# Accumulating scatters of a top-2 mixture of experts, placed one at a time; another form for the last expert

## The chip, the core and the metric

One NeuronCore of a Trainium2 chip runs the whole program. The metric is the device time of one execution in microseconds, the median of several runs. TensorE (PE) multiplies matrices, VectorE (DVE) and ScalarE (ACT) work elementwise, GpSimd (POOL) computes elementwise as well and issues the DMAs whose rows are chosen by an index (gathers and scatters), and SyncE (SP) issues the other DMAs. Each engine takes its own instructions strictly in order.

## The reference, cut to what matters

Attention and a gated feed-forward layer give 2304 tokens of 512 numbers. A mixture of eight experts follows; every token goes to two of them, and the result of a token is the weighted sum of the two:

```python
top2 = np.argpartition(-noisy_logits, 2, axis=1)[:, :2]
...
out = np.zeros((N, D), dtype=np.float32)
for e in range(E):
    for k in range(2):
        mask = top2[:, k] == e
        ...
        h = np.maximum(x[mask] @ w1[e], 0.0)
        out[mask] += top2_w[mask, k, None] * (h @ w2[e])
```

Here E is 8, x[mask] has 512 columns, w1[e] is 512 x 1024 and w2[e] is 1024 x 512.

## The kernel before, in words

The gate scatters each token's row, its weights and its number into `xs`, a region in device memory for each expert (`g_scatter`, L620, plain scatters of 96 rows). An expert then has up to 640 of its rows in five tiles of 128 (the fifth has 104 for experts 2 to 7).

Experts 0 and 1 are done in 32 units (`units`, L1151): 16 slices of 128 hidden columns in two parts of the tokens, "a" with three tiles and "b" with two. Units 0 to 7 are expert 0's part a, 8 to 15 expert 1's a, 16 to 23 expert 1's b, 24 to 31 expert 0's b. A unit makes the up products of its slice (`up2`), the down products of the unit before (`down2`), and splits the weights of the unit two ahead into a high and a low half (`prep2`, ACT then DVE).

Experts 2 to 7 are done in 24 pairs of slices (`pair`, L1068), four to an expert. A pair multiplies two slices at once in a Strassen-like scheme of seven products (`product`, L1048), which needs sums and differences of weight blocks (`sums_ws`, on POOL, L1010 to L1013) and of the turned rows (`sums_xs`, on POOL), split into halves by ACT (`high_ws`, L1028) and DVE (`low_ws`, L1032). Among the products stand the down products of the pair before (`down_s`, L1062). The sums for pair p + 1 are issued at the start of pair p.

An expert's five tiles sum in five banks of PSUM. `finish` (L920) multiplies a tile by the tokens' weights into a buffer `pv`, and `add` (L931) issues a scatter on POOL that adds the 128 rows into `out` in device memory. Every scatter into `out` waits until the one before has landed, since the rows of two may be the same. For experts 2 to 6 `finish` runs in the first pair of the next expert, and issues its scatters at once: three, then two.

Side work has its place by hand: `put(("u", n), h, fn, ...)` or `then` places a call in unit n at step h, `at(p, h, fn, ...)` in pair p, and `run` issues what is due, in the order of h.

Of the kernel before, what the change touches and what calls it, by code (L numbers as in the profile page):

```python
# [14 lines left out]
AF = mybir.ActivationFunctionType  # L15
OP = mybir.AluOpType
# [8 lines left out]
E = 8  # L25
# [31 lines left out]
NC = CAP // 128  # L57
# [10 lines left out]
def moe_program(ctx, tc, phi, kv, q, wa, wgn, nz, wb, out):  # L68
# [10 lines left out]
    V, A, P, G, Q = nc.vector, nc.scalar, nc.tensor, nc.gpsimd, nc.sync  # L79
# [560 lines left out]
    def put(i, n, fn, *a):  # L640
        fill.setdefault((i, n), []).append((fn, a))
# [38 lines left out]
    for b in range(1, B):  # L680
        i = 2 * b - 2
        n = AT["s1"][min(b, 2)]
# [187 lines left out]
    def rows(e, part):  # L870
        if "all" not in PV:
            PV["all"] = wpool.tile([128, 8, DM], F32, tag="X0", name="pv", bufs=1)
            PV["next"], PV["ring"] = 0, 3
        for t in TILES[part]:
            PV[e, t] = PV["all"][:, PV["next"], :]
            PV["next"] = (PV["next"] + 1) % PV["ring"]
# [40 lines left out]
    def height(e, t):  # L917
        return CAPS - 128 * t if e > 1 and t == NC - 1 else 128

    def finish(e, tiles, late=False, engines="AV"):  # L920
        ml = ML[e]
        for t in tiles:
            pv, h = PV[e, t], height(e, t)
            if engines[t % len(engines)] == "V":
                V.tensor_scalar(pv[:h], AC2[e, t][:h], ml[:h, t, e:e + 1], None, op0=OP.mult)
            else:
                A.activation(pv[:h], AC2[e, t][:h], AF.Copy, scale=ml[:h, t, e:e + 1])  # L927
            if not late:
                add(e, t)

    def add(e, t):  # L931

        h = height(e, t)
        G.indirect_dma_start(out=out, out_offset=bass.IndirectOffsetOnAxis(ap=IX[e][:h, t:t + 1], axis=0),  # L934
                             in_=PV[e, t][:h], in_offset=None, compute_op=OP.add)


    A11, A12, A22, S1, S2, S3, S4 = range(7)
# [113 lines left out]
    def down_s(p, n, tiles):  # L1052
        e, f = 2 + p // 4, 2 * (p % 4) + n
        hh, hl = HS[p, n]
        w = W2[24 + 2 * p + n]
        for t in tiles:
            h = height(e, t)
            if f == 0:
                AC2[e, t] = bank((0, 1, 4, 2, 3)[t], [128, DM], "acc")
            o = slice(128 * t, 128 * t + h)  # L1060
            for m, (a, b) in enumerate(((hh, 0), (hh, 1), (hl, 0))):
                P.matmul(AC2[e, t][:h], r(a[:, o]), r(w[:, b]), start=(f == 0 and m == 0),  # L1062
                         stop=(f == NF2 - 1 and m == 2))
# [95 lines left out]
    def then(s, f, part, half, fn, *a):  # L1159
        put(("u", pos[s, f, part]), half, fn, *a)  # L1160

    def then_x(s, f, part, e, k, a):
        then(s, f, part, 1, trans_x, e, k, a)
        then(s, f, part, 2.1, split_x2, e, k, a)
# [9 lines left out]
        then(0, 6 + k // 2, "a", 1.5 * (k % 2), trans_x, 1, k, "a")  # L1174
        then(0, 6 + k // 2, "a", (1, 2.1)[k % 2], split_x2, 1, k, "a")
    then(1, 0, "a", 1, index, 1, "a")
    then(1, 0, "a", 1.5, finish, 0, TILES["a"], True)
    for t in TILES["a"]:
        then(1, (0, 1, 1)[t], "a", (1.6, 0.5, 1.5)[t], add, 0, t)
    then(1, 2, "a", 0.5, rows, 1, "a")  # L1180
    put(("u", 10), 0.3, swap)
    put(("u", 10), 0.3, load_x, 1, "b")
    then(1, 5, "a", 2.1, index, 1, "b")
    for k in range(4):
        then(1, 6 + k // 2, "a", (1, 2.1)[k % 2], trans_x, 1, k, "b")
        then(1, 6 + k // 2, "a", (1.5, 2.2)[k % 2], split_x2, 1, k, "b")
    put(("u", 16), 0, open_s1)
    then(1, 0, "b", 1, load_x, 0, "b")
    then(1, 0, "b", 1.5, finish, 1, TILES["a"])
# [6 lines left out]
    then(2, 2, "b", 1.5, rows, 0, "b")  # L1196
    then(1, 0, "b", 1, load_xs, 2)
    for k in range(2):
        for n, (f, fn, m) in enumerate(((20, trans_xs, 0), (20, trans_xs, 1), (21, sums_xs, 0), (21, None, 0),
                                        (22, None, 1), (22, None, 2), (22, sums_xs, 1), (23, None, 3))):  # L1200
            f += (0, 4 + (n > 3))[k]
            h = (1, 2.1, 0.1, 1, 1, 1.1, 2.3, 1)[n]
            if fn:
                put(("u", f), h, fn, 2, k, m)
            else:
                put(("u", f), h, high_xs, 2, k, m)
                put(("u", f), h + 1.1, low_xs, 2, k, m)
# [6 lines left out]
    def at(p, h, fn, *a):  # L1214
        put(("s", p), h, fn, *a)

    pairs = 4 * (E - 2)
# [49 lines left out]
    open_s2()  # L1267
    for p in range(pairs):
        e, q = 2 + p // 4, p % 4
        if p == 0:  # L1270
            def first(h):
                if h == 0:
                    down2(*units[-1])
                    finish(0, TILES["b"], engines="A")
                    rows(2, "ab")

            def second(h):
                pass
        else:
            ends = p % 4 == 0  # L1280

            def first(h):
                down_s(p - 1, 0, (range(3), range(3, NC))[h])

            def second(h):
                t = (range(3), range(3, NC))[h]
                down_s(p - 1, 1, t)
                if ends:
                    finish(e - 1, t, engines="A")
                    if h:  # L1290
                        rows(e, "ab")
        pair(p, first, second)
    for t in range(NC):
        for n in range(2):
            down_s(pairs - 1, n, (t,))
        finish(E - 1, (t,), engines="AV")
    assert not fill, fill
    right.close()
    left.close()
# [78 lines left out]
```

## Time and profile before

| what | value |
|---|---|
| median of 3 runs | 998.56 us (997.41 to 999.58) |
| the profiled execution, its own time | 997.44 us |
| its span, first to last instruction | 995.6 us |
| PE busy | 852.6 us (86%) |
| DVE busy | 626.4 us (63%) |
| ACT busy | 394.8 us (40%) |
| POOL busy | 322.0 us (32%) |
| mean granted clock of TensorE | 0.933 of full speed |

The busy times are shares of the whole span. The attention and the first layer take the first 420 us or so, the units of experts 0 and 1 run from there to about 554 us, and the pairs from 554 us to the end.

### The profile page before, as it was taken

The numbers are of one execution on the slowest core, as the hardware profiler recorded it, in microseconds if no ns is written. First come the engines' busy times: TensorE is split into PE (matmuls) and PEld (weight loads), VectorE is DVE, ScalarE is ACT, GpSimd is POOL, SyncE is SP. The second block draws the span as 40 slices with busy tenths as digits, with TensorE's granted clock in tenths as the row PEclk, the third lists the DMA queues.
The fourth block names the chain that finished last, engine by engine and source line by source line (L and its number), as shares of the span: only waits on it lengthen the run. The fifth ranks groups of instructions, "written<-read, shape, count | busy, mean of one in ns | idle before, by whom it ended". The sixth has DMA issues, their size and how long they took to land. (4 is left out here: it accounts for less than half of the span.)

```text
span 995.6 us, 16514 instructions
## 1 busy us (share of the span) xinstructions
PE 852.6 (86%) x6136; PEld 746.5 (75%) x6136; DVE 626.4 (63%) x1498; ACT 394.8 (40%) x845; POOL 322.0 (32%) x438
## 2 busy tenths in 40 slices
PE   5989999999999999999897799579499399399490
PEld 2768888998999889887787688468378288288380
DVE  4775686767767685866465688278187187285340
ACT  3754554334433433434353445145145145244220
POOL 2000114242424244223224254353453442542302
PEclk9999999999999999999989899879889699699695
DMA  9966378753445346656692526417427237224203
GB/s 335 400 250 178 104 241 292 247 142 96 138 138 147 85 138 189 184 157 208 173 234 43 127 76 140 91 44 153 79 70 159 46 95 150 30 86 107 29 12 43
DMA packets 85002, 140.76 MB, mean 141 GB/s; under 512 B 16352, under 2 KB 41152, under 8 KB 84912
## 3 DMA queue, kind: packets, MB, share of 16 engines
q1 hardware_dynamic: 65712, 100.66, 33.1%
q0 software_dynamic: 19200, 38.96, 17.8%
q8 instruction: 50, 0.82, 0.3%
q14 instruction: 40, 0.33, 0.1%
HBM read 102.81 MB, written 36.77 MB: 140 GB/s over the span
## 5 line engine op out<-in xcount | busy, mean ns | idle before, releaser
L1048 PE MATMUL ph<-xh,ws 128*128 128x308 f32 x1008 | 168.4, 312 | 85.4 <-ACT ws L1028 71.2
L1048 PEld LDWEIGHTS ph<-xh,ws 128*128 128x128 f32 x1008 | 155.6, 193 | 101.1 <-ACT ws L1028 72.5
L1062 PE MATMUL acc<-ws,hs 128*128 128x512 f32 (+1 forms) x720 | 191.3, 409 | 0.0
L1062 PEld LDWEIGHTS acc<-ws,hs 128*128 128x128 f32 (+1 forms) x720 | 135.4, 194 | 27.5
L934 POOL DMA_INDIRECT out<-pv,ix x40 | 64.3, 1608 | 217.1 <-DMA out<-pv,ix 96.5
L459 PE MATMUL acc<-a,ro 128*128 128x288 f32 x576 | 116.3, 294 | 0.0
L426 PE MATMUL pg<-x,pt 128*128 128x288 f32 x576 | 103.3, 314 | 6.4 <-ACT pt L394 4.4
L459 PE MATMUL acc<-a,os 128*128 128x288 f32 x432 | 105.8, 294 | 0.8 <-DVE os L408 0.8
L1066 DVE SCALAR_TENSOR_TENSOR hs<-y,hs 128x308 fp32r<-128x308 f32 x72 | 42.7, 598 | 93.0 <-ACT hs L1104 89.8
L426 PEld LDWEIGHTS pg<-x,pt 128*128 128x128 f32 x576 | 82.3, 191 | 25.0 <-issue 7.6
L426 PE MATMUL pv<-x,pt 128*128 128x288 f32 x576 | 93.3, 298 | 0.0
L459 PEld LDWEIGHTS acc<-a,ro 128*128 128x128 f32 x576 | 92.1, 188 | 0.0
L426 PEld LDWEIGHTS pv<-x,pt 128*128 128x128 f32 x576 | 83.0, 191 | 0.0
L439 DVE SCALAR_TENSOR_TENSOR ta<-ta,pg 128x288 f32<-128x288 f32 x84 | 37.9, 451 | 66.5 <-ACT ta L434 61.7
L622 POOL DMA_INDIRECT xs<-R,gidx x48 | 49.0, 1022 | 89.5 <-DMA xs<-R,gidx 84.6
L418 POOL DMA_DIRECT2D os<-osl x72 | 40.6, 564 | 106.2 <-PE acc L459 62.7
L459 PEld LDWEIGHTS acc<-a,os 128*128 128x128 f32 x432 | 74.1, 188 | 1.1 <-DVE os L408 1.1
L434 ACT ACTIVATE ta<-pg 128x288 f32<-128x288 f32 x84 | 34.4, 410 | 88.2 <-PE pg L426 86.2
L1028 ACT ACTIVATE ws<-ts 128x512 fp32r<-128x512 f32 x46 | 28.6, 622 | 102.5 <-POOL ts L1011 102.3
L445 ACT ACTIVATE a<-ta 128x288 fp32r<-128x288 f32 x84 | 37.4, 445 | 72.1 <-DVE ta L440 66.2
L896 PE MATMUL ph<-xt,wm 128*128 128x384 f32 (+1 forms) x256 | 60.5, 322 | 5.6 <-ACT xt L858 4.0
L896 PEld LDWEIGHTS ph<-xt,wm 128*128 128x128 f32 x256 | 45.9, 195 | 11.2 <-ACT xt L858 6.0
(212 smaller groups left out, 1512.0 us busy)
## 6 DMA issues: line engine op xcount, KB each, us to landing
wb<-wb SPq DMA_DIRECT2D x72, 512.0 KB
os<-osl POOLq DMA_DIRECT2D x72, 256.0 KB, 3.5
stg<-wa SPq DMA_DIRECT2D x19, 511.8 KB
kv<-kv SPq DMA_DIRECT2D x32, 256.0 KB
xl<-xs SPq DMA_DIRECT2D x40, 160.0 KB
out<-zt SPq DMA_DIRECT2D x1, 5888.0 KB
xd<-R SPq DMA_DIRECT2D x8, 603.0 KB
qt<-q SPq DMA_DIRECT2D x8, 576.0 KB
```

What stands on the lines that cost most here:

```text
L418: G.dma_start(r(lo), r(osl[f][:, :]))
L426: P.matmul(p, r(PT[f // 2, g][:, w, f % 2, 128 * a:128 * a + 128]), r(X[i][:, s, g, :]), start=(g == 0 and n == 0), stop=(g == 1 and n == 2))
L434: A.activation(ta, pg, AF.Tanh, scale=0.5)
L439: V.scalar_tensor_tensor(ta, ta, 1.0, pg, op0=OP.add, op1=OP.mult)
L445: A.activation(r(ah[:, 0, :]), ta, AF.Copy)
L459: P.matmul(ACC[i][c], r(OS[i, f][w][:, o]), r(ah[:, s, :]), start=(f == 0 and n == 0), stop=(f == NF1 - 1 and n == 2))
L622: G.indirect_dma_start(out=xs[:, :], out_offset=bass.IndirectOffsetOnAxis(ap=RT[i][:, t, n:n + 1], axis=0), in_=R[i][:, t, :], in_offset=None)
L896: P.matmul(p, r(w[:, c]), r(x[:, k, b, :]), start=(m == 0), stop=(m == 11))
L934: G.indirect_dma_start(out=out, out_offset=bass.IndirectOffsetOnAxis(ap=IX[e][:h, t:t + 1], axis=0), in_=PV[e, t][:h], in_offset=None, com ...
L1048: P.matmul(out, r(w[:, i, c + 128 * k:c + 128 * k + 128]), r(x[:, m, k, a]), start=(start and n == 0), stop=(n == 5), skip_group_check=not ...
L1062: P.matmul(AC2[e, t][:h], r(a[:, o]), r(w[:, b]), start=(f == 0 and m == 0), stop=(f == NF2 - 1 and m == 2))
L1066: V.scalar_tensor_tensor(r(hl), y, 0.0, hh, op0=OP.max, op1=OP.subtract)
```

## The change

`finish` no longer issues scatters. It puts the tile on a list `todo`, and `add()` without arguments takes the oldest from it and issues its scatter. Eight such calls stand in the units (8, twice in 9, then 17, 19, 21, 27, 29), and two in every pair, at steps 2.5 and 5.9. All tiles are now scaled by ACT, where some were scaled by DVE.

The last expert is treated otherwise. In pair 23 five gathers (`gather`) read from `out` the rows to which its five tiles belong. At the end `finish` multiplies a tile by the weights and adds the gathered rows in one DVE instruction, and a plain scatter (`OP.bypass`) writes the sum to `out`. The down products of pair 22 for tiles 3 and 4 are held back from pair 23 to the very end, after the down products of pair 23 for tiles 0 to 2.

Two placements of other work move as well. The turned rows of expert 1's part b (`trans_x`, `split_x2`) go from units 14 and 15, two in each, to units 12 to 15, one in each. Some transposes, sums and splits of expert 2's rows in units 20 to 29 move by up to one unit.

```diff
-    def finish(e, tiles, late=False, engines="AV"):
+    todo = []
+
+    def finish(e, tiles):
         ml = ML[e]
         for t in tiles:
-            pv, h = PV[e, t], height(e, t)
-            if engines[t % len(engines)] == "V":
-                V.tensor_scalar(pv[:h], AC2[e, t][:h], ml[:h, t, e:e + 1], None, op0=OP.mult)
-            else:
-                A.activation(pv[:h], AC2[e, t][:h], AF.Copy, scale=ml[:h, t, e:e + 1])
-            if not late:
-                add(e, t)
-
-    def add(e, t):
-
-        h = height(e, t)
-        G.indirect_dma_start(out=out, out_offset=bass.IndirectOffsetOnAxis(ap=IX[e][:h, t:t + 1], axis=0),
-                             in_=PV[e, t][:h], in_offset=None, compute_op=OP.add)
+            pv, h = PV[e, t][:height(e, t)], height(e, t)
+            w = ml[:h, t, e:e + 1]
+            if e == E - 1:
+                V.scalar_tensor_tensor(pv, AC2[e, t][:h], w, pv, op0=OP.mult, op1=OP.add)
+                add(e, t)
+                continue
+            A.activation(pv, AC2[e, t][:h], AF.Copy, scale=w)
+            todo.append((e, t))
+
+    def add(*tile):
+        if tile or todo:
+            e, t = tile or todo.pop(0)
+            h = height(e, t)
+            G.indirect_dma_start(out=out, out_offset=bass.IndirectOffsetOnAxis(ap=IX[e][:h, t:t + 1], axis=0),
+                                 in_=PV[e, t][:h], in_offset=None, compute_op=OP.bypass if tile else OP.add)
+
+    def gather(e):
+        for t in range(NC):
+            h = height(e, t)
+            G.indirect_dma_start(out=PV[e, t][:h], out_offset=None, in_=out,
+                                 in_offset=bass.IndirectOffsetOnAxis(ap=IX[e][:h, t:t + 1], axis=0))
...
-    then(1, 0, "a", 1.5, finish, 0, TILES["a"], True)
-    for t in TILES["a"]:
-        then(1, (0, 1, 1)[t], "a", (1.6, 0.5, 1.5)[t], add, 0, t)
+    then(1, 0, "a", 1.5, finish, 0, TILES["a"])
+    for u, h in ((8, 1.6), (9, 0.5), (9, 1.5), (17, 0.5), (19, 0.5), (21, 0.5), (27, 0.5), (29, 0.5)):
+        put(("u", u), h, add)
...
     for k in range(4):
-        then(1, 6 + k // 2, "a", (1, 2.1)[k % 2], trans_x, 1, k, "b")
-        then(1, 6 + k // 2, "a", (1.5, 2.2)[k % 2], split_x2, 1, k, "b")
+        then_x(1, 4 + k, "a", 1, k, "b")
...
     for k in range(2):
-        for n, (f, fn, m) in enumerate(((20, trans_xs, 0), (20, trans_xs, 1), (21, sums_xs, 0), (21, None, 0),
-                                        (22, None, 1), (22, None, 2), (22, sums_xs, 1), (23, None, 3))):
-            f += (0, 4 + (n > 3))[k]
-            h = (1, 2.1, 0.1, 1, 1, 1.1, 2.3, 1)[n]
+        for f, h, fn, m in (((20, 1, trans_xs, 0), (20, 2.1, trans_xs, 1), (20, 2.2, sums_xs, 0), (21, 1, None, 0),
+                             (22, 1, None, 1), (22, 1.1, None, 2), (22, 2.3, sums_xs, 1), (24, 1, None, 3)),
+                            ((24, 2.2, trans_xs, 0), (25, 1, trans_xs, 1), (25, 2.3, sums_xs, 0), (26, 1, None, 0),
+                             (27, 1, None, 1), (27, 1.1, None, 2), (27, 2.3, sums_xs, 1), (29, 1, None, 3)))[k]:
...
         e, q = 2 + p // 4, p % 4
+        at(p, 2.5, add)
+        at(p, 5.9, add)
         if p == 0:
...
         else:
-            ends = p % 4 == 0
+            ends, held = q == 0, p == pairs - 1
 
             def first(h):
-                down_s(p - 1, 0, (range(3), range(3, NC))[h])
+                down_s(p - 1, 0, (range(3), range(3, 3 if held else NC))[h])
 
             def second(h):
-                t = (range(3), range(3, NC))[h]
-                down_s(p - 1, 1, t)
+                t = (range(1), range(1, 3)) if held else (range(3), range(3, NC))
+                down_s(p - 1, 1, t[h])
                 if ends:
-                    finish(e - 1, t, engines="A")
+                    finish(e - 1, t[h])
                     if h:
                         rows(e, "ab")
+        if p == pairs - 1:
+            at(p, 2.6, gather, E - 1)
         pair(p, first, second)
+    p = pairs - 1
+    down_s(p, 0, range(3))
     for t in range(NC):
-        for n in range(2):
-            down_s(pairs - 1, n, (t,))
-        finish(E - 1, (t,), engines="AV")
+        if t > 2:
+            for n in range(2):
+                down_s(p - 1, n, (t,))
+            down_s(p, 0, (t,))
+        down_s(p, 1, (t,))
+        finish(E - 1, (t,))
+    assert not todo
```

## Rows read from the trace of the kernel before

**Rows 1.** Costliest groups: line, engine, operation, busy us, mean ns, idle before, releaser.

```profile
L1048 PE MATMUL ph<-xh,ws 128*128 128x308 f32 x1008 | 168.4, 312 | 85.4 <-ACT ws L1028 71.2
...
L934 POOL DMA_INDIRECT out<-pv,ix x40 | 64.3, 1608 | 217.1 <-DMA out<-pv,ix 96.5
...
L1066 DVE SCALAR_TENSOR_TENSOR hs<-y,hs 128x308 fp32r<-128x308 f32 x72 | 42.7, 598 | 93.0 <-ACT hs L1104 89.8
```

**Rows 2.** Who waited for whom, 600 to 996 us: total us, times, longest.

```profile
ACT ws L1028 <- POOL ts L1011: 100.7, 5, 20.6
```

**Rows 3.** Timeline of POOL and once ACT: start us, us, instruction, idle before.

```profile
543.28 1.56 POOL L934 DMA_INDIRECT out<-pv,ix  x1 [3.79 <-DMA out<-pv,ix]
...
668.83 1.30 POOL L1011 TENSOR_TENSOR ts<-wb 128x256 f32<-128x256 f32 x1
...
685.86 0.62 ACT L1028 ACTIVATE ws<-ts 128x512 fp32r<-128x512 f32 x1
...
690.98 1.70 POOL L934 DMA_INDIRECT out<-pv,ix  x1 [7.78 <-ACT pv L927]
...
696.54 1.56 POOL L934 DMA_INDIRECT out<-pv,ix  x1 [3.86 <-ACT ws L1028]
...
704.06 1.54 POOL L934 DMA_INDIRECT out<-pv,ix  x1 [5.96 <-DMA out<-pv,ix]
...
714.67 1.60 POOL L934 DMA_INDIRECT out<-pv,ix  x1 [3.77 <-DMA out<-pv,ix]
...
718.02 0.72 POOL L1010 TENSOR_TENSOR ts<-wb 128x256 f32<-128x256 f32 x1
```

**Rows 4.** Windows: five pairs with a wait (first, sum), three without (sum).

```profile
635.26:667.36 32.10, 15.94 (x73) 13.45 (x72) 14.49 (x26) 8.90 (x19) 15.19 (x16) 0.73 0.25 54
...
sum 159.21, PE 80.00 PEld 67.41 DVE 69.78 ACT 43.26 POOL 70.58; mean PE 16.00 PEld 13.48 DVE 13.96 ACT 8.65 POOL 14.12
...
sum 39.16, PE 39.05 PEld 34.37 DVE 28.33 ACT 18.59 POOL 15.50; mean PE 13.02 PEld 11.46 DVE 9.44 ACT 6.20 POOL 5.17
```

**Rows 5.** Timeline of all engines in the tail, 960 to 996 us.

```profile
962.35 8.48 PE L1062 MATMUL acc<-ws,hs 128*128 128x512 f32 x36
...
965.33 0.69 ACT L927 ACTIVATE pv<-acc,ml 128x512 f32<-128x512 f32 x1 [1.80 <-PE acc L1062]
966.29 1.58 POOL L934 DMA_INDIRECT out<-pv,ix  x1 [26.74 <-ACT pv L927]
...
988.12 1.61 POOL L934 DMA_INDIRECT out<-pv,ix  x1 [4.09 <-DMA out<-pv,ix]
```

**Rows 6.** Windows in the units: us, busy of PE, PEld, DVE, ACT, POOL, clock.

```profile
494.00:506.00 12.00, 9.00 (x33) 7.21 (x34) 5.29 (x11) 5.05 (x9) 1.57 (x1) 0.72 0.83 183
542.00:554.00 12.00, 7.64 (x38) 6.36 (x37) 2.83 (x7) 3.45 (x8) 3.21 (x3) 0.86 0.17 23
```

**Rows 7.** Timelines of DVE, SP's queue and PE, 479 to 488 us.

```profile
479.01 0.56 DVE L900 SCALAR_TENSOR_TENSOR hl<-ph,hh 128x384 fp32r<-128x384 f32 x1 [1.92 <-ACT hh L899]
479.96 0.69 DVE L779 TENSOR_TENSOR ro<-wb,wm 128x512 fp32r<-128x512 f32 x1 [0.39 <-ACT wm L778]
...
482.19 1.80 SPq L844 DMA_DIRECT2D xl<-xs  x4
...
484.84 0.34 PE L896 MATMUL ph<-xt,ro 128*128 128x384 f32 x1
...
487.11 0.17 DVE L865 SCALAR_TENSOR_TENSOR iu<-ml,c_off 128x2 f32<-128x2 f32 x1 [1.69 <-DMA ml<-xs]
```

**Rows 8.** Timeline of POOL: two plain scatters of the gate.

```profile
465.13 0.92 POOL L622 DMA_INDIRECT xs<-R,gidx  x1 [2.57 <-DMA xs<-R,gidx]
468.17 1.44 POOL L622 DMA_INDIRECT xs<-R,gidx  x1 [2.11 <-DMA xs<-R,gidx]
```

**Rows 9.** The plain scatters of L622, all 48: issue to landing.

```profile
DMA to landing us min/median/max: 2.8/3.0/7.1
```

**Rows 10.** The accumulating scatters of L934, all 40: issue to landing.

```profile
DMA to landing us min/median/max: 4.5/4.9/9.1
```

More of the change, by code (lines that the diff above doesn't have):

```diff
@@ L1273, in first @@
                     down2(*units[-1])
-                    finish(0, TILES["b"], engines="A")
+                    finish(0, TILES["b"])
                     rows(2, "ab")
```

## The prediction

> **What bounds the kernel now.** I read the page's costliest groups first. TensorE's up products of the last six experts (L1048) are busy for 168.4 us and idle for 85.4 us, of which 71.2 us end with a copy of weights on ACT; the accumulating scatters (L934) made POOL wait 96.5 us for the landing of an earlier one [rows 1]. The table of waits of the last 400 us then names what ACT waits for: POOL's weight sums, five times, 20 us each [rows 2]. So I read POOL's timeline at one of the five places [rows 3]. When an expert is finished, its five scatters stand in POOL's queue together. Each waits until the one before has landed: the spacing is 7.5 us (696.54 to 704.06) while weights are being loaded, some 5.3 us (704.06 to 714.67 in two steps) afterwards. Behind the fifth stand the weight sums of L1010, which start at 718.02. The pair of slices that needs them began at 706.52.
>
> The windows give the price. The five pairs that hold such a wait take 159.21 us, TensorE is busy for 80.00 of them, and the granted clock of the first is 0.73, so part of the rest runs at the lower of the clock's two levels (1.2 against 2.4 GHz). Three pairs in a row without one take 39.16 us, 13.05 each, with TensorE busy for 39.05 and a granted clock of 1.00 [rows 4]. In the tail, TensorE's last products start at 962.35 and last 8.48 us, and the last five scatters then run one by one from 966.29 to the end of the span at 995.6 [rows 5].
>
> **The five boundaries.** After the change POOL issues one scatter late in the pair in which the expert is finished and two in each of the next two. The ordering wait stays, but what stands between two scatters is now other work. I lay the pairs of [rows 3] out with the new order, at 13.05 us a pair from 680.42. Tile 0 goes at 691; two slice sums and four weight sums (0.72 to 1.30 us each) follow and end by 699.7; tile 1 goes there, since tile 0 needs 5.6 us. Tile 2 follows at 707.2 if I charge the loaded 7.5 us. The next weight sums then run from 708.8 to 712.4; their first half, done at 710.4, is copied by ACT 5.4 us into the pair (685.86 in the one from 680.42), so at 711.9. Tile 3 goes at 714.7, tile 4 at 722.2, and the weight sums behind it have their first half at 725.4, where ACT asks at 725.0; TensorE reads the first of them only in the pair from 732.7. So I cost the waits that remain at nothing: the copies of the next pair's weights cover them by several us of TensorE's time. The sum for five pairs is 5 x 13.05 = 65.3 against 159.21: **-93.9 us**. That this rate holds for longer than three pairs is the assumption; a bound above is 5 us for each expert (a rival, below).
>
> Spread out, the scatters run beside a busy DVE, where the last three of a group stood beside an idle one. The first scatter of [rows 3], beside a busy DVE (28.33 of 39.16 us in [rows 4]), lasts 1.70 us, a later one, with DVE idle, 1.54: 0.16 us for each of 25, hidden. The Trainium skill (SBUF — State Buffer, SBUF: two separate sides) says that descriptors of POOL's DMAs cannot be written while a DVE instruction in a two-port mode holds the shared port. By that the scatters would become POOL's largest work, which the 0.16 us do not bear out; what it would do here is rival (d).
>
> **The units before (L1174 to L1212).** Two stalls lie there. From 542 to 554 TensorE is busy 7.64 of 12 us at a granted clock of 0.86: 4.36 us idle, and 7.64 x 0.14 = 1.1 us lost to the clock, 5.4 us in all [rows 6]. Inside it a scatter that waited for the one before goes only at 543.28 [rows 3], and POOL's slice sums stand behind it. The change puts these two scatters a unit and a half apart, behind which no sums wait: **-5.4 us**; below, 0, if the sums are late for another reason. The stretch 494 to 506 has 3.0 us idle and 9.0 x 0.28 = 2.5 us of clock, 5.5 in all [rows 6]; there the turned rows of expert 1's second part come late. The change turns them two units earlier, one in each of units 12 to 15. But their load is issued from 482.19, behind the scatters of the gate, and DVE's next wait on it ends at 487.11. Unit 12's place in DVE's queue is behind 479.01. DVE would stand there for 7.5 us, and with it the low half of the weights (L779, now at 479.96) that TensorE reads at 484.84 [rows 7]. That is 3.4 us of idle TensorE (484.8 to 488.2) and, as in [rows 6], about 2 us of clock. So a stall of 5.4 us appears at unit 14 and the one of 5.5 at unit 16 goes: **0**, with bounds of -5.5 (the load is in time) and +6 (both remain). Making ACT write all three tiles of a first finish, in place of one on DVE, moves 0.7 us of work to an engine idle for most of the units: nothing. The other moved transposes of expert 2 keep their order; nothing, or 1 us either way.
>
> **The tail.** The scatters of expert 6 all go before pair 23 now, and POOL, which has no sums left there, issues five gathers: 5 x 1.7 us by the longest scatter of [rows 3], under a pair of 13 us, read only after the last products. Twelve down products of pair 22 move behind pair 23. From the 36 products of [rows 5], one takes 8.48/36 = 0.235 us. Pair 23's last up product is thus 2.8 us earlier, and tile 0 needs 18 products after it where it needed 12: its finish comes 2.8 - 1.4 = 1.4 us earlier. DVE's multiply-add in place of ACT's 0.69 us copy (965.33) costs at most 0.3 us more (598 ns at 308 columns in [rows 1], scaled to 512). Then five plain scatters. I take it that they wait for each other as the plain scatters of the gate do (465.13, 468.17 in [rows 8]); their landing is 3.0 us for 96 rows [rows 9] against 4.9 for the accumulating ones of 128 [rows 10]. Scaled by rows it is between 3.0 and 4.0; I take 3.4, and with the 0.7 us from landing to next issue a spacing of 4.1. Before, four spacings were 988.12 - 966.29 = 21.8 us, and 7.5 us lay behind the last; now 16.4 and 6.3 (1.2 less landing). 1.1 + 5.4 + 1.2 = **-7.7 us**. Bounds: -1.1 if plain ones cost the same, and -17 if they don't wait for each other (TensorE then ends the work 7 us after tile 0's finish: 1.1 + 14.8 + 1.2). The Trainium skill (DMA: Bandwidth & Descriptors, Anatomy of one DMA) fits such a DMA as 2.0 us and bytes by 436 GB/s: 2.6 us for these 262 KB, an estimate by which the tail would end 4 us sooner still; the measured 3.0 for a smaller one speaks for the longer.
>
> **Sum.** -93.9 - 5.4 + 0 - 7.7 = -107.0 us. The profiled execution took 997.4 us (span 995.6, 1.8 around it), the median is 998.6; from the median I get 998.6 - 107.0 = **891.6**, in a profiled span of 888.6.
>
> **Rivals.** (a) Landings beside loads are long: 9.1 us is the longest of [rows 10]. With 9.8 us of spacing, tile 4 goes at 729.1, its sums end at 734.3, and their copies at 735.6, where TensorE wants them at 733.5; with ACT held back before, some 5 us for each of five experts: 917. The 7.5 us of all the loaded pairs of [rows 3] is against it. Chance 0.09. (b) The turned rows block and unit 16's stall stays: 6 us more, 898; the wait at 487.11 is for it, the freed units 14 and 15 against. Chance 0.09. (c) The last scatters don't wait for each other: 882; against it the gate's. Chance 0.08. (d) The descriptors wait for DVE: with POOL served only in DVE's idle 28 per cent, a scatter of 1.54 us takes 1.54/0.28 = 5.5, and a pair with two holds 11.0 us of scatters, 4.5 of weight sums and 2 of slice sums, 4.4 over 13.05; ten such pairs, +44: 936. The 1.70 us above is against it. Chance 0.03. (e) Slower: each of the 25 scatters inside pairs keeps TensorE waiting for the 7.5 us to its landing, since the weight sums are needed at once: +188, 1079. It decides from 4.3 us per scatter on (107/25). Against it: the sums serve the pair after, as laid out. Chance 0.02. (f) The scatters still bunch, as an earlier queue entry holds POOL, and nothing changes: 998; against it, POOL is busy 15.50 of 39.16 us in unstalled pairs. Chance 0.01. My forecast has 0.67 and a range of its own of 882 to 901 (the bounds of tail and units); the last 0.01 lies between.
>
> **Range and chances.** 877 to 908 holds the forecast, (b) and (c): 0.84, with the ends set a little outside (c) and (b). The three runs of before lie 0.2% apart, and less than that can't be told from no change. Faster 0.97, within it 0.01, slower 0.02.
>
> **What would show it.** In the new profile the five boundaries have no idle time of TensorE before L1048 put down to ACT's copies, pairs of 13.05 us at a granted clock of 1.00, and POOL's scatters two to a pair with waits that end before the sums are wanted; 542 to 554 is full; a wait of DVE on expert 1's load stands near unit 12, and TensorE idles some 3 us at unit 14; the last five scatters stand 4.1 us apart. Wrong would be: pairs longer than 13.05 throughout, weight copies that still wait for POOL, or final scatters as far apart as the accumulating ones.

## The result, and the profile after

The changed kernel takes 894.54 us (median of 4 runs, 890.83 to 897.41) against 998.91 us for the kernel before, measured beside it: a ratio of 0.8955 [0.8912, 0.8998]. The forecast was 891.6, in a range of 877 to 908. A second measurement gave 897.59 us and 0.8962 [0.8942, 0.8982]. The profiled execution took 897.11 us, with a span of 895.3 and a granted clock of 0.983; of the four it is one of the two longer ones.

First the costliest groups of the changed kernel, by form (busy us, mean ns, idle before, releasers), as in [rows 1]:

```profile
L1058 PE MATMUL ph<-xh,ws 128*128 128x308 f32 x1008 | 165.0, 308 | 10.2 <-DVE ws L1042 4.4 <-DVE u L1096 3.3 <-DVE v L1103 1.7
...
L938 POOL DMA_INDIRECT out<-pv,ix x40 | 65.1, 1629 | 109.0 <-ACT pv L931 57.9 <-DMA out<-pv,ix 21.4 <-DVE pv L928 10.8
...
L1076 DVE SCALAR_TENSOR_TENSOR hs<-y,hs 128x308 fp32r<-128x308 f32 x72 | 50.9, 707 | 3.4 <-ACT hs L1123 0.5
...
L1038 ACT ACTIVATE ws<-ts 128x512 fp32r<-128x512 f32 x46 | 28.5, 621 | 0.9 <-POOL ts L1021 0.9
...
L1042 DVE TENSOR_TENSOR ws<-wb,ws 128x512 fp32r<-128x512 f32 x24 | 23.9, 996 | 0.0
```

The 85.4 us in which the up products stood still are 10.2 now, and ACT's copy of weights is gone from their releasers, and that copy itself waits 0.9 us for POOL in all; POOL's wait for an earlier scatter is 21.4 us where it was 96.5. Two things are new in these lines. The releasers that are left are all DVE's, and DVE's instructions have become longer: hs<-y,hs takes 707 ns where it took 598 [rows 1]. The same view of the kernel before has for the last two of the lines:

```profile
L1028 ACT ACTIVATE ws<-ts 128x512 fp32r<-128x512 f32 x46 | 28.6, 622 | 102.5 <-POOL ts L1011 102.3
...
L1032 DVE TENSOR_TENSOR ws<-wb,ws 128x512 fp32r<-128x512 f32 x24 | 17.2, 716 | 0.0
```

POOL's timeline at one boundary of the changed kernel (start, us, instruction, idle before), as in [rows 3]:

```profile
614.82 1.69 POOL L938 DMA_INDIRECT out<-pv,ix  x1 [7.85 <-ACT pv L931]
...
620.17 1.19 POOL L1020 TENSOR_TENSOR ts<-wb 128x256 f32<-128x256 f32 x1
...
625.06 1.61 POOL L938 DMA_INDIRECT out<-pv,ix  x1 [0.16 <-issue]
...
631.76 1.55 POOL L938 DMA_INDIRECT out<-pv,ix  x1 [0.16 <-issue]
632.78 1.32 POOL L1020 TENSOR_TENSOR ts<-wb 128x256 f32<-128x256 f32 x1
...
637.49 1.82 POOL L938 DMA_INDIRECT out<-pv,ix  x1 [0.16 <-issue]
```

Scatter and sums alternate. When a scatter's turn comes, the one ahead has landed, and it goes 0.16 us after the instruction in front of it. The first of the five waits for its own tile. It is so at the four boundaries from pair 4 to pair 19 (waits of 0.15 to 0.19 us behind the first). The other scatters inside the pairs that still wait stand elsewhere: one behind pair 0, at 565.36, for 7.83 us, and two of expert 6's, at 843.06 and 853.70, for 3.92 and 3.22.

The windows of seven whole pairs (us; busy PE, PEld, DVE, ACT, POOL; granted clock), the four of one expert and then the last expert's first to third, of which two are left out; the rows to set beside them are [rows 4]:

```profile
658.25:671.11 12.86, 12.86 (x74) 11.45 (x73) 9.41 (x18) 7.44 (x16) 3.64 (x3) 1.00 0.53 120
671.11:684.96 13.85, 13.38 (x74) 11.47 (x72) 13.47 (x21) 7.53 (x16) 10.18 (x9) 1.00 0.52 113
684.96:698.41 13.45, 13.14 (x73) 11.47 (x72) 11.53 (x20) 5.97 (x13) 9.62 (x9) 1.00 0.54 118
698.41:712.23 13.82, 13.39 (x73) 11.47 (x72) 12.92 (x19) 6.61 (x15) 9.46 (x10) 1.00 0.70 158
820.25:833.16 12.91, 12.91 (x74) 11.48 (x72) 9.21 (x17) 7.43 (x16) 4.21 (x5) 1.00 0.27 81
```

The clock is full throughout. A pair takes 12.9 us where DVE has no more than 9.4 us to do (in one of the two left out POOL is busy for 8.75 us even so), and 13.5 to 13.9 where DVE is busy for 11.5 to 13.5 us and POOL for some 10.

In the units, the windows as in [rows 6]:

```profile
485.00:497.00 12.00, 6.87 (x29) 6.17 (x28) 6.94 (x16) 4.01 (x7) 1.60 (x1) 0.86 0.90 240
494.00:506.00 12.00, 11.98 (x67) 10.60 (x66) 5.91 (x13) 7.49 (x13) 1.58 (x1) 1.00 0.67 196
...
540.00:552.00 12.00, 12.00 (x75) 10.58 (x73) 4.49 (x9) 3.31 (x9) 2.56 (x3) 1.00 0.19 27
```

DVE's wait in the first of these windows, and TensorE's stop behind it, from the timelines:

```profile
489.48 0.45 DVE L853 STREAM_TRANSPOSE xu<-xl 128x256 f32<-128x256 f32 x1 [9.49 <-DMA ml<-xs]
...
490.55 0.69 PE L896 MATMUL ph<-xt,ro 128*128 128x384 f32 x1 [5.13 <-DVE ro L779]
```

The stall of unit 16 and the one at 542 are gone, and one stands at unit 14, where the low half of the weights (L779) is behind the turned rows in DVE's queue. And the last five scatters of the changed kernel on POOL, as in [rows 5]:

```profile
873.08 1.02 POOL L938 DMA_INDIRECT out<-pv,ix  x1 [8.26 <-DVE pv L928]
876.63 0.97 POOL L938 DMA_INDIRECT out<-pv,ix  x1 [2.54 <-DMA out<-pv,ix]
...
887.17 1.01 POOL L938 DMA_INDIRECT out<-pv,ix  x1 [2.59 <-DMA out<-pv,ix]
```

They do wait for each other, 3.52 us apart in the mean where the accumulating ones were 5.46 apart.

Cut at the same instructions, the two profiled executions compare as follows (us; the units begin with the first product of L896, pairs with their first up product):

| stretch | before | after | difference | forecast |
|---|---|---|---|---|
| up to the units | 418.06 | 419.90 | +1.8 | 0 |
| units | 136.29 | 128.90 | -7.4 | -5.4 |
| pairs 0 to 5 | 80.91 | 82.17 | +1.3 | 0 |
| pairs 6 to 22 | 315.59 | 227.99 | -87.6 | -93.9 |
| pair 23 to the end | 44.75 | 36.34 | -8.4 | -7.7 |
| span | 995.6 | 895.3 | -100.3 | -107.0 |

Pairs 6 to 22 as one window, first before and then after (columns as above), show where most of it went, the idle time of TensorE and the lower clock:

```profile
635.26:950.85 315.59, 236.05 (x1226) 204.92 (x1224) 182.04 (x313) 116.62 (x243) 131.83 (x126) 0.85 0.39 85
```

```profile
630.97:858.96 227.99, 223.71 (x1225) 195.07 (x1224) 193.96 (x307) 113.99 (x237) 137.09 (x121) 1.00 0.52 118
```

### The profile page after: what moved, and what is told of

It is laid out like the page before. It is cut to its first block, busy times and chain, and to the rows that moved or that the text cites. A ratio compares the mean times of both kernels' runs of the same rounds, so it can differ in the third digit from the quotient of the medians.

```text
span 895.3 us, 16500 instructions
## 1 busy us (share of the span) xinstructions
PE 837.7 (94%) x6136; PEld 735.6 (82%) x6136; DVE 644.1 (72%) x1498; ACT 394.5 (44%) x845; POOL 336.1 (38%) x443
## 4 chain that ended last, share of the span: by engine, by line
PE 65%; DVE 13%; DMA 11%; issue 5%; ACT 3%; POOL 1%; SPq 1%; DVEq 0%; POOLq 0%; ACTq 0%
PE acc L459 13%; PE acc L1072 12%; PE ph L1058 11%; PE pg L426 9%; PE pv L426 7%; DMA xs<-R,gidx 4%; PE ph L896 3%; PE acc L914 3%; PE acc L455 2%; PE pp L314 2%; DVE ws L1049 2%; DVE xh L1005 2%; DMA out<-pv,ix 1%; DVE ws L1042 1%; PE pT L481 1%
## 5 line engine op out<-in xcount | busy, mean ns | idle before, releaser
L1072 PE MATMUL acc<-ws,hs 128*128 128x512 f32 (+1 forms) x720 | 183.1, 396 | 0.0
L1058 PE MATMUL ph<-xh,ws 128*128 128x308 f32 x1008 | 165.0, 308 | 10.2 <-DVE ws L1042 4.4
L1058 PEld LDWEIGHTS ph<-xh,ws 128*128 128x128 f32 x1008 | 152.3, 189 | 25.7 <-DVE ws L1042 6.1
L1072 PEld LDWEIGHTS acc<-ws,hs 128*128 128x128 f32 (+1 forms) x720 | 129.5, 186 | 25.7
L622 POOL DMA_INDIRECT xs<-R,gidx x48 | 49.0, 1021 | 88.4 <-DMA xs<-R,gidx 83.2
L896 PE MATMUL ph<-xt,wm 128*128 128x384 f32 (+1 forms) x256 | 59.1, 318 | 2.3 <-ACT xt L858 1.1
L1076 DVE SCALAR_TENSOR_TENSOR hs<-y,hs 128x308 fp32r<-128x308 f32 x72 | 50.9, 707 | 3.4 <-ACT hs L1123 0.5
L896 PEld LDWEIGHTS ph<-xt,wm 128*128 128x128 f32 x256 | 45.1, 193 | 6.6 <-ACT xt L858 2.2
L896 PE MATMUL ph<-xt,ro 128*128 128x384 f32 (+1 forms) x128 | 40.5, 317 | 5.2 <-DVE ro L779 5.1
```

The lines of the kernel that those rows point to most:

```text
L622: G.indirect_dma_start(out=xs[:, :], out_offset=bass.IndirectOffsetOnAxis(ap=RT[i][:, t, n:n + 1], axis=0), in_=R[i][:, t, :], in_offset=None)
L896: P.matmul(p, r(w[:, c]), r(x[:, k, b, :]), start=(m == 0), stop=(m == 11))
L1058: P.matmul(out, r(w[:, i, c + 128 * k:c + 128 * k + 128]), r(x[:, m, k, a]), start=(start and n == 0), stop=(n == 5), skip_group_check=not ...
L1076: V.scalar_tensor_tensor(r(hl), y, 0.0, hh, op0=OP.max, op1=OP.subtract)
```

## Experiments

My theory: the boundaries were lost to the order of POOL's queue and to nothing else, and the 6.3 us by which the pairs fall short of the forecast come from DVE's instructions being lengthened by POOL's sums beside them. The rivals are told with each run.

**The order in POOL's queue.** The changed kernel, with the scatters of experts 2 to 6 issued at the finish, as before:

```
             todo.append((e, t))
+            if 1 < e:
+                add()
```

> The changed kernel, but the five scatters of each of the experts 2 to 6 are issued at once when the expert is finished, as before; everything else stays changed. Theory (queue order): the weight sums stand again behind five landings in POOL's queue, the five pairs take about 32 us in place of 13.5, so +92 us: about 985 us. Rival (the gain came mostly from the last expert and the units): at most +30 us, below 925 us.

Measured: 983.45 us, 0.9846 [0.9820, 0.9871]. Its page shows the old groups again, and its waits (total us, times, longest) have the row of [rows 2], with the same total:

```profile
L1060 PE MATMUL ph<-xh,ws 128*128 128x308 f32 x1008 | 169.7, 314 | 85.0 <-ACT ws L1040 71.1
...
L1078 DVE SCALAR_TENSOR_TENSOR hs<-y,hs 128x308 fp32r<-128x308 f32 x72 | 42.6, 597 | 92.9 <-ACT hs L1116 89.7
```

```profile
ACT ws L1040 <- POOL ts L1023: 100.7, 5, 20.7
```

So one placement, of 25 instructions that all still run, is worth 0.9846 - 0.8955 = 0.089 of the time, some 89 us of the 104; pairs 6 to 22 take 316.5 us again. The mean of hs<-y,hs is back at 597 ns with it.

**POOL's sums as the cause of the longer pairs.** The sums are replaced by fills with zero from expert 3's slices and pair 5's weights on: this kernel leaves out part of the computation, its scatters stay.

```
+        if e > 2:
+            if m == 0:
+                G.memset(u, 0.0)
+            return
 ...
+        if p > 4:
+            G.memset(c, 0.0)
+            G.memset(d, 0.0)
+            return
```

> The changed kernel, but POOL's sums of weights (from pair 5 on) and of rows (experts 3 to 7) are replaced by fills with zero, so that POOL reads nothing from SBUF in the pairs; the products are made from the wrong numbers, in the same count. Theory (DVE's instructions with two SBUF inputs are slowed while POOL reads SBUF): the multiply-subtract of L1076 falls from 707 ns to below 600, and the pairs from 13.5 to 12.9 us each, 10 us less in all: about 885 us. Rival (the scatters slow DVE, or DVE simply has too many instructions): pairs stay at 13.4 to 13.5 us and the time within 3 us.

Measured: 886.62 us (2 runs), 0.8867 [0.8838, 0.8896]. The windows of one expert's second and third pair, and the group of hs<-y,hs:

```profile
668.25:681.51 13.26, 13.15 (x74) 11.46 (x72) 10.52 (x21) 7.77 (x17) 5.17 (x7) 1.00 0.65 131
681.51:694.37 12.86, 12.86 (x74) 11.44 (x72) 9.63 (x20) 5.63 (x13) 4.87 (x5) 1.00 0.53 128
```

```profile
L1084 DVE SCALAR_TENSOR_TENSOR hs<-y,hs 128x308 fp32r<-128x308 f32 x72 | 35.1, 488 | 3.9 <-ACT hs L1131 0.5
```

An expert takes 51.8 us (four windows) where the changed kernel needs 54.0, and the instruction is down to 488 ns. DVE has the same work in number, 21 and 20 instructions in these two windows as in the changed kernel's; it is the time of each that changes. Pairs 6 to 22 take 220.2 us in place of 228.0.

**The scatters as the cause.** The rival: the scatters between the pairs' work make them longer. The 25 scatters of experts 2 to 6 are left out, so those experts' results are not added.

```
-            todo.append((e, t))
+            if e < 2:
+                todo.append((e, t))
```

> The changed kernel, but the 25 scatters of the experts 2 to 6 are left out, so their results are missing from the output. Theory (POOL's sums slow DVE, the scatters do not): pairs stay at 13.4 to 13.5 us and the time within 3 us of the changed kernel. Rival (the scatters' descriptors or landings cost the half microsecond of each pair): pairs fall to 12.9 us and the time by 8 us.

Measured: 889.35 us (2 runs), 0.8895 [0.8860, 0.8929], and 53.4 us for an expert.

```profile
L1077 DVE SCALAR_TENSOR_TENSOR hs<-y,hs 128x308 fp32r<-128x308 f32 x72 | 44.8, 623 | 3.8 <-ACT hs L1124 0.5
```

Taking the scatters away gives 0.6 us an expert, taking the sums away 2.2; over pairs 6 to 22 it is 2.5 us and 7.8. The sums are the larger cause. The median is 5.2 us below the changed kernel's first one, more than the 3 us expected: half of it is gained from pair 23 on, where the span ends 5.4 us behind the start of the last scatter in place of 8.2.

The scatters are not quite free, and the kept traces show where. A scatter alone does not lengthen the instruction: laid beside POOL's timeline, 47 of the 72 hs<-y,hs of the changed kernel stand beside nothing of POOL and take 467 to 483 ns, 4 beside a scatter alone take 472 to 479, and 21 beside a sum take 1008 to 2067. In the fourth pair of an expert the instruction starts beside a scatter whose sums follow at once. There it lasts 2.07 us, and 1.01 in the kernel without the scatters (POOL and DVE of the changed kernel, then DVE of the other):

```profile
644.95 1.83 POOL L938 DMA_INDIRECT out<-pv,ix  x1 [0.19 <-issue]
646.23 1.32 POOL L1020 TENSOR_TENSOR ts<-wb 128x256 f32<-128x256 f32 x1
```

```profile
645.93 2.07 DVE L1076 SCALAR_TENSOR_TENSOR hs<-y,hs 128x308 fp32r<-128x308 f32 x1
```

```profile
646.00 1.01 DVE L1077 SCALAR_TENSOR_TENSOR hs<-y,hs 128x308 fp32r<-128x308 f32 x1
```

That pair takes 13.8 us with the scatter in front of the sums and 13.05 without; the second pair is the same in both, 13.9, and the third 0.15 longer without them. Why a scatter and the sums behind it together hold the instruction for so long is open.

**The last expert's kind of scatter.** Expert 7 by accumulating scatters, without gathers and with ACT's finish:

```
-                V.scalar_tensor_tensor(pv, AC2[e, t][:h], w, pv, op0=OP.mult, op1=OP.add)
+                A.activation(pv, AC2[e, t][:h], AF.Copy, scale=w)
 ...
-                                 in_=PV[e, t][:h], in_offset=None, compute_op=OP.bypass if tile else OP.add)
+                                 in_=PV[e, t][:h], in_offset=None, compute_op=OP.add)
 ...
-        if p == pairs - 1:
-            at(p, 2.6, gather, E - 1)
```

> The changed kernel, but the last expert's tiles are scaled by ACT and added to the output by accumulating scatters, with no gathers; the order of the products stays changed. Theory: only the spacing of the last five scatters changes, from 3.5 us back to 5.5 us, so +8 us: about 902 us. Rival (the tail gained by its earlier start alone): the same time within 2 us.

Measured: 903.69 us, 0.9043 [0.9020, 0.9065]. POOL's first and last scatter of the tail:

```profile
871.79 1.57 POOL L938 DMA_INDIRECT out<-pv,ix  x1 [15.21 <-ACT pv L928]
...
894.33 1.60 POOL L938 DMA_INDIRECT out<-pv,ix  x1 [4.17 <-DMA out<-pv,ix]
```

Four spacings are 22.5 us against 14.1 in the changed kernel, so the plain write saves 8.4 us there, close to the 9.1 between the medians. The gathers that make it possible lie under pair 23: tile 0's scatter goes 14.0 us into the pair without them and 14.1 with them. What they may cost stands behind the last scatter, 0.4 us (the part on the tail, below).

**The same kernel again, the turned rows, and the held products.** These were timed side by side, with the version after them. The first is the changed kernel itself:

> The changed kernel itself, as the measure of the three beside it on the same chip: 891 to 897 us, by all theories.

Measured: 897.59 us (894.52 to 898.87), 0.8962 [0.8942, 0.8982]. In the second the transposes of expert 1's turned rows stay at units 14 and 15:

```
-        then_x(1, 4 + k, "a", 1, k, "b")
+        then(1, 6 + k // 2, "a", (1, 2.1)[k % 2], trans_x, 1, k, "b")
+        then(1, 6 + k // 2, "a", (1.5, 2.2)[k % 2], split_x2, 1, k, "b")
```

> The changed kernel, but the turned rows of expert 1's second part go back to units 14 and 15. Theory (the move trades one stall for another): the 5 us stall at unit 14 goes and the 5.5 us one at unit 16 returns, so the time stays within 1.5 us of the changed kernel. Rival (the move was worth the stall that it removes): 5 us slower. Second rival (the move only costs): 5 us faster.

Measured: 893.84 us, 0.8924 [0.8906, 0.8943]. Its windows of the units (columns as before) show the stall where the kernel before had it:

```profile
485.00:497.00 12.00, 10.21 (x53) 8.86 (x51) 7.25 (x16) 4.13 (x7) 0.00 (x0) 1.00 0.82 249
494.00:506.00 12.00, 9.05 (x42) 7.16 (x41) 5.09 (x12) 6.42 (x10) 1.58 (x1) 0.86 0.84 178
```

The medians say 3.75 us in favour of late, more than the 1.5 us expected, but the profiles do not find them: the units take 127.85 us against 129.17 in the run above, and the spans are 892.1 and 892.7 (the profiled execution of the run above was its shortest). A later pair (below) settles it as far as it was settled.

In the third no down products are held back: those of the last pair but one for tiles 3 and 4 are done inside the last pair, and the tiles are ended in their old order.

```
-            ends, held = q == 0, p == pairs - 1
+            ends, held = q == 0, False
 ...
-    down_s(p, 0, range(3))
     for t in range(NC):
-        if t > 2:
-            for n in range(2):
-                down_s(p - 1, n, (t,))
-            down_s(p, 0, (t,))
-        down_s(p, 1, (t,))
+        for n in range(2):
+            down_s(p, n, (t,))
         finish(E - 1, (t,))
```

> The changed kernel, but the twelve down products of pair 22 for tiles 3 and 4 stay inside pair 23, and the tiles are ended in their old order. Theory (the chain of five final scatters sets the end, and the order only moves its start by 1.4 us): 1 to 2 us slower. Rival (TensorE's end sets the time): the same, since the products are as many.

Measured: 900.41 us, 0.8996 [0.8974, 0.9017]. Its last pair begins at 856.40:

```profile
871.91 1.02 POOL L938 DMA_INDIRECT out<-pv,ix  x1 [8.51 <-DVE pv L928]
877.47 0.96 POOL L938 DMA_INDIRECT out<-pv,ix  x1 [4.54 <-DVE pv L928]
881.22 0.96 POOL L938 DMA_INDIRECT out<-pv,ix  x1 [2.79 <-DMA out<-pv,ix]
```

Tile 0's scatter goes 15.5 us into the pair where it went 14.1, and the second has to wait for its tile's finish (5.56 us behind the first). Holding back products is worth 2.8 us by the medians and 3.6 by the profiles from pair 22 on, more than the 1 to 2 expected; the two intervals still touch.

**A version meant to be better.** Three edits together: expert 0's scatters at units 11 to 13 and the turned rows from unit 13 on; the row work of the next expert spread more evenly over its four pairs, and out of the way in pair 0; and the end tile by tile with only tile 0 ahead.

```
-    for u, h in ((8, 1.6), (9, 0.5), (9, 1.5), (17, 0.5), ...
+    for u, h in ((11, 0.5), (12, 0.5), (13, 0.5), (17, 0.5), ...
 ...
+            if p == 0:
+                t = ((6.8, trans_xs, 0, 0), (6.8, trans_xs, 0, 1), (6.85, sums_xs, 0, 0))
 ...
-                t = (range(1), range(1, 3)) if held else (range(3), range(3, NC))
+                t = (range(1), ()) if held else (range(3), range(3, NC))
```

> Three further moves on the changed kernel, the output whole: (1) the scatters of expert 0's first part go two or three units later, so that the gate's last scatters and the load behind them are not held up, and the turned rows stand where that load has landed, in units 13 to 15; (2) in the pairs the splitting of the next expert's rows is spread more evenly over DVE's four pairs, and in pair 0 the transposes that wait for a load stand behind the weights of pair 1; (3) at the end tile 0 is finished first, with the products of tiles 1 to 4 held back. Theory, from the stalls of the changed kernel's profile: -5 us in the units, -3 us in the pairs, -5 us at pair 0, -2.8 us in the tail: some 880 us. Rival (each stall only moves): within 3 us of the changed kernel.

Measured: 896.12 us (890.65 to 899.40, 6 runs), 0.8949 [0.8925, 0.8973]: a miss, and the rival holds, since the changed kernel beside it took 897.59. The profiled one (890.65 us) shows which parts fell. In the units the stall moved from unit 14 to units 16 to 19, and they take 128.0 us against 129.2. Pairs 6 to 21 take 215.7 us against 215.1: spreading the row work gives nothing. The changed kernel has a stop of 4.38 us early in pair 1, where DVE's weights stand behind transposes placed in pair 0 that wait for a load (its last part lands at 560.73, they start at 561.00). It is 0.93 us here, but further on in the same pair stands one of 4.17, for a reason that POOL's and ACT's timelines name:

```profile
561.24 1.85 POOL L938 DMA_INDIRECT out<-pv,ix  x1 [7.91 <-DMA out<-pv,ix]
562.55 1.41 POOL L987 TENSOR_TENSOR sx<-xr 128x308 f32<-128x308 f32 x1
```

```profile
564.90 0.72 ACT L1001 ACTIVATE xh<-sx 128x616 fp32r<-128x616 f32 x1 [5.29 <-POOL sx L988]
```

It is the change's own subject once more: a scatter that waits 7.9 us for the one ahead, and slice sums behind it. Only the end got shorter, from pair 22 on 46.8 us against 49.0.

**Its parts, taken apart.** Three kernels timed side by side. The end alone:

```
-                t = (range(1), range(1, 3)) if held else (range(3), range(3, NC))
+                t = (range(1), ()) if held else (range(3), range(3, NC))
 ...
     for t in range(NC):
+        for n in range(2):
+            if t == 0:
+                down_s(p - 1, n, (1,))
+            elif t > 1:
+                down_s(p - 1, n, (t,))
+        for n in range(2):
+            down_s(p, n, (t,))
         finish(E - 1, (t,))
```

> The changed kernel with another order at its end: of the last two pairs' down products only tile 0's are done inside the last pair, and tiles 1 to 4, of both pairs, behind it, tile by tile. If the end is set by a chain of five scatters of about 3.5 us each that starts with tile 0's finish, what counts is only when tile 0 is finished, and this is to end 2 to 3 us earlier than the changed kernel (about 893 us beside a kernel before of 1000), with the five scatters still 3.5 us apart and the first of them some 11.5 us behind the last pair's first product instead of 14.1. Rival: the products are what sets the end, tile 4's finish moves back as far as tile 0's moves forward, and the time stays within 1 us.

Measured: 892.48 us, 0.8916 [0.8897, 0.8934]. The last pair begins at 858.03 in its profile, and the first two scatters are:

```profile
869.35 1.02 POOL L938 DMA_INDIRECT out<-pv,ix  x1 [4.92 <-DVE pv L928]
872.91 0.96 POOL L938 DMA_INDIRECT out<-pv,ix  x1 [2.54 <-DMA out<-pv,ix]
```

That is 11.3 us into the pair, as expected, and the stretch from pair 22 on is 47.3 us against 49.0 to 49.3. The last two spacings were 3.9 and 4.0 us here, which took part of it back. The end is a chain of scatters; what counts is when the first can go. With the first scatter 2.8 us earlier in its pair than in the changed kernel this end is 1.7 to 2.0 us shorter; with it 1.4 us later, in the kernel without held products, where the second was late as well, it was 3.6 longer.

With the turned rows late as well:

```
-        then_x(1, 4 + k, "a", 1, k, "b")
+        then(1, 6 + k // 2, "a", (1, 2.1)[k % 2], trans_x, 1, k, "b")
+        then(1, 6 + k // 2, "a", (1.5, 2.2)[k % 2], split_x2, 1, k, "b")
```

> Both: the transposes of expert 1's turned rows at units 14 and 15, where the kernel before had them, and the end by tile 0 first. If moving those transposes to units 12 and 13 cost the change 1.5 to 4 us (the units took 120.0 us with them late and 121.3 to 121.6 with them early, in three profiles), this is to be that much below the run with the end alone. Rival: the units' lengths scatter by as much from run to run by themselves, and the two are within 1 us.

Measured: 893.34 us, 0.8931 [0.8914, 0.8949]: no gain beside 892.48. From the first product of the units to the first pair, the profiles with the rows early have 126.89 to 130.25 us (eight of them), with them late 127.85, 128.45 and 127.57 (the last from the run below); the lengths in the expectation are of a cut some 8 us shorter. The 3.75 us of the earlier measurement were not found again; the rival holds.

And with the first pair cleared:

```
+                if p == 0:
+                    h = 6.8 if fn is trans_xs else 6.85
                 at(p, h, fn, e + 1, k, m)
 ...
-        at(p, 5.9, add)
+        if p:
+            at(p, 5.9, add)
```

> As the run before, and in the first pair the second scatter is left to a later pair and the transposes of expert 3's rows come behind the last weight split. In the changed kernel TensorE stands 4.4 us in that pair. Theory: it is one more case of work that stands in line behind a wait, on VectorE behind the transposes (they wait for a load) and on GpSimd the slice sums behind a scatter that waits 7.8 us for the one ahead; with both out of the way the stop of 4.4 us falls under 1.5 us and the time by 3 to 4 us. Rival: the loads of that stretch are late by themselves, something else is waited for in the same place, and the time stays within 1 us.

Measured: 892.35 us (888.51 to 893.08), 0.8911 [0.8888, 0.8934]. TensorE's stop in pair 1 of the changed kernel, and the stops in that pair here:

```profile
563.20 1.40 PE L1058 MATMUL ph<-xh,ws 128*128 128x308 f32 x4 [4.38 <-DVE ws L1042]
```

```profile
557.33 0.83 PE L1058 MATMUL ph<-xh,ws 128*128 128x308 f32 x4 [0.93 <-DVE ws L1042]
...
562.24 1.11 PE L1058 MATMUL ph<-xh,ws 128*128 128x308 f32 x6 [1.16 <-DVE u L1096]
...
566.81 1.13 PE L1058 MATMUL ph<-xh,ws 128*128 128x308 f32 x6 [1.23 <-DVE v L1103]
```

The stop of 4.38 us became three of 0.93, 1.16 and 1.23, and pairs 0 to 5 take 79.1 us against 82.1 in the run ahead of it and 80.8 to 82.5 in every other profile here. With the transposes alone out of the way (the version meant to be better) the stop moved on; with the scatter out of the way too, none over 1.3 us is left. The theory holds for the place; the median fell by only 1.0 us, within what runs of one kernel differ by, where 3 to 4 were expected. This kernel and the one with the end alone lie some 0.5% below the changed one (0.8911 and 0.8916 against 0.8955 and 0.8962) and so below both; they were not timed beside it, and the interval of its first measurement still touches theirs.

## Why the prediction was right, point by point

**The five boundaries: mechanism right, size 6.3 us short.** POOL's queue was the cause; putting the old order back costs 89 us. The copies of weights wait 0.9 us for POOL in all where it was 102.3, as laid out, and the clock came back to 1.00. What was mis-sized is the rate. I took 13.05 us a pair from three windows and named its holding as the assumption. Over pairs 6 to 22 it was 227.99/17 = 13.41. Two of the three windows of [rows 4] were pairs in which POOL did little:

```profile
680.42:706.52 26.10, 25.99 (x146) 22.91 (x144) 16.56 (x30) 11.98 (x25) 7.50 (x6) 1.00 0.59 127
```

Only 1.4 of the 6.3 us lie in the five pairs themselves, which take 66.6 us against the 65.3 forecast. The rest is in pairs beside them, which I left at their length before: the one ahead of a boundary went from 13.25 to 13.85, the one behind it from 13.06 to 13.84. Without stalls, POOL's sums fall less into DVE's idle time and more beside its work: from pair 6 to 22, DVE's instructions with both inputs in SBUF ran beside a sum for 59.6 us before and 92.9 after. Over the kernel hs<-y,hs went from 598 to 707 ns, ws<-wb,ws from 716 to 996; DVE's instructions that read one input from PSUM did not change (u<-ph,s 470 and 468 ns). The Trainium skill (SBUF — State Buffer, Who interferes with whom) says that a DVE instruction with two SBUF inputs contends with a GpSimd instruction that reads SBUF, and not with one that only writes it. The trace agrees in both: with fills in the place of sums, hs<-y,hs took 488 ns and an expert 2.2 us less. I had weighed the scatters beside DVE, and not the sums.

**Units: -7.4 against -5.4.** The stall at 542 went, and gave more than costed: units 24 to 31, which held it, take 22.6 us in place of 29.3, so 6.7 against 5.4. No run puts the old order of the scatters back in the units alone, and some of expert 2's row work moved there too, so which of the two did it is argued, not shown. The turned rows did what was forecast, to the unit: DVE stood until 489.48, TensorE stopped 5.1 us at unit 14 (3.4 forecast), and unit 16's stall went. The term of 0 is borne out by the runs with the rows late, which differ by no more than the profiles do among themselves. So rival (b), that both stalls remain, is refuted.

**Tail: -8.4 against -7.7.** Tile 0's scatter goes 1.3 us earlier within its pair (1.1 forecast), and the spacing is 3.52 and not 4.1 us, so four of them give -7.7 in place of -5.4: a landing took 2.7 us where I had 3.4. Behind the start of the last scatter lie 8.2 us where I expected 6.3 and the kernel before had 7.5. That step was wrong in kind. I took 1.2 us off for the shorter landing (by my own figures 4.9 - 3.4 = 1.5), as if the landing ended the span. It doesn't: the last landing is at 890.4, 4.9 us before the end, and what runs on is a closing instruction in POOL's queue, DRAIN. The view of its line has (three of them; shortest, median and longest in ns, start of the first and the last), first before, then after:

```profile
L1374 POOLq DRAIN  x3: 46/107/3739, 991.1 to 995.4; - x3
```

```profile
L1393 POOLq DRAIN  x3: 46/106/4148, 890.3 to 895.0; - x3
```

It starts some 3 us behind the start of the last scatter in both and lasts 3.74 us before and 4.15 after. It is 3.74 in the run with accumulating scatters and no gathers too, 4.15 in all runs that have the gathers and all the scatters, and 3.41 with 25 scatters fewer; what sets it is open. That the two errors of the tail nearly cancel is luck. The Trainium skill (DMA: Bandwidth & Descriptors, Anatomy of one DMA) gave 2.6 us for such a transfer, an estimate; the trace is nearer to that, with 2.7 us for the shortest landing and 2.54 us of POOL's wait, than to my 3.4. Rival (c), no wait between the last scatters, is refuted by that wait.

**The other rivals.** (a) and (d) would have shown scatters that go late; at the boundaries those behind the first go 0.15 to 0.19 us after their turn, land in 4.5 to 5.9 us, and take 1.55 to 1.85 us each beside a busy DVE. Inside the pairs a landing as long as (a) wants was seen once, behind pair 0: 8.9 us, and the next scatter waited 7.83. (e) and (f) are refuted by the time.

**What no term held.** The stretch up to the units, which the change doesn't touch, was 1.8 us longer in this execution, and its end lies between 416.6 and 419.9 us over all the profiles of this study. Pairs 0 to 5 took 1.3 us more; 0.6 of it is pair 5, the one ahead of the first of the five. The median lies 2.9 us from the forecast and the profiled span 6.7 from its 888.6, so the closeness of the median is in part luck: the four executions span 6.6 us. The inner range's upper end of 901 is not worked out in the prediction; its bounds give 898 one at a time and 904 together.

## What to carry to other kernels

An engine that runs in order and also issues transfers that wait for each other is a place where independent work is held up: look for what stands behind the waiting instruction, and put one transfer at a time between pieces of that work, at least a landing apart. When a stall goes, the rate of the stretches without it is too good a forecast if they also had less work beside them; take it from a stretch with the full load. A chain of ordered writes at the end is shortened by finishing its first link early and by making each link cheaper.

## What the runs showed that I had not expected

An accumulating scatter of 128 rows costs 5.5 us a link in a chain, a plain one to the same rows 3.5, with 1.57 and 0.97 us of POOL's own time; reading the rows back first cost next to nothing under other work. A fill on POOL left DVE's two-input instruction hs<-y,hs at 488 ns in the mean where sums on POOL made it 707; beside a sum a single one takes 1.0 to 2.1 us, beside a scatter alone 0.48. And the span does not end with the last landing: POOL's closing DRAIN of 3.7 to 4.2 us does not get shorter with it.
